# Seven block products for eight in the first matrix product of pairs of token blocks

## Chip, core and metric

One core of one Trainium2 chip. The metric is the time of the whole kernel on the device in microseconds, the median of three runs. TensorE (PE in the profile; PEld is its weight load) multiplies, VectorE (DVE), ScalarE (ACT) and GpSimd (POOL) do the elementwise work, SyncE (SP) issues the DMAs in order.

## The reference

Block-sparse attention on 4 x 8 heads of 768 tokens with 64 dimensions, and on its output a mixture of four experts, each applied to every token:

```python
scores_all = np.concatenate([scores_l_m, scores_s], axis=-1)   # window of 16, and block maxima of k
a = np.exp(scores_all - max) / (sum + 1e-09)
x = np.matmul(a, np.concatenate([v, v_sum], axis=2))           # -> (3072, 512)
p = domain_probs / (domain_probs.sum(-1, keepdims=True) + 1e-09)
for e in range(4):
    h = np.maximum(x @ w1[e], 0.0)                             # 512 -> 1024
    out += p[:, e:e + 1] * (h @ w2[e])                         # 1024 -> 512
```

Everything is float32.

## The kernel before

Tokens are cut into eight blocks of 384 (`TB`). Attention makes x transposed, in 64 steps `n` (eight for a block: four pieces of 96 queries, two groups of heads); a step is `load_piece`, `stage_a`, two `scores`, `probs`, `transposed` (a transposing DMA), `values` and `to_x`, the last of which writes x of its columns.

Matrix operands are split in two parts of type fp32r, a rounded high part and the remainder (xh and xl, wh and wl, hh and hl), and a product is three matmuls: high by high, high by low, low by high. ScalarE makes the high part, GpSimd or VectorE the low one (`split_weights`).

A pass of one expert over one or two blocks is `moe_units` (L620). Its first product, `mm1`, takes for each of 8 columns blocks `fc` of w1 (128 wide) and each token block 4 chunks of the depth (128 each) x 3 matmuls of 128x384 into one PSUM bank `ph`, 12 in all. ScalarE then takes the positive part (hh, `AF.Relu`), VectorE the remainder (hl). The second product, `mm2`, takes per 128 tokens 8 x 3 matmuls of 128x512 into a bank `po`, which VectorE scales by the expert's weight and adds to `acc`; after the fourth expert SP stores it. The pool `ps_mm` has four PSUM banks for ph and po; scores and values have two each. w1 and w2 are loaded and split anew in every pass; four w1 columns blocks and all of w2 are kept where the next pass has the same expert.

The order: `plan` (L720) has block 0 with experts 0 and 1, block 1 with experts 1 and 0, blocks 0 and 1 with experts 2 and 3, then the pairs (2,3), (4,5), (6,7) with all four experts, twelve passes in three stages. Passes give units, and after each unit `advance` lets so many attention steps be issued that they are spread evenly over the stage. The first attention steps are written out with keys of their own (`first_tokens`). Behind these the order of instructions on each engine is worked out by the planner of the tile framework, which simulates a timeline and takes what is ready by program order; tiles of one tag share a number of slots, and what needs a slot waits for the release of an earlier tile. Nearly all instructions have the line of the helper `issue`, L73, so groups are told apart by tiles.

Of the kernel before, what the change touches and what calls it, by code (L numbers as in the profile page):

```python
# [16 lines left out]
P = 128  # L17
# [19 lines left out]
LAG = 2.52  # L37
PACE = 1.013
# [4 lines left out]
STEPS = (-1.19, -0.88, 0.85, 0.66, 1.27, 1.34, 1.82, 1.84, 3.16, 3.29, 3.37, 3.66, 3.72, 5.09, 5.84, 6.11, 6.57, 6.89)  # L43
ASC = 32768.0
# [16 lines left out]
def attn_moe(ctx: ExitStack, tc: tile.TileContext, qvL, qv0, v0L, kD, kT, vT, w1L, w2L, dpL, cst, out):  # L61
# [28 lines left out]
    ps_av = pool("ps_av", 2, space=bass.MemoryType.PSUM)  # L90

# [8 lines left out]
    dp = const.tile([P, NT, E], F32, name="dp")  # L100
    pw = const.tile([P, NT, E], F32, name="pw")

    def mixing():
        SP.dma_start(dp, dpL)
        s = const.tile([P, NT, 1], F32, name="dps")
        V.tensor_reduce(s, dp, axis=AX.X, op=ALU.add)
        V.tensor_scalar_add(s, s, EPS)
        r = const.tile([P, NT, 1], F32, name="dpr")
        V.reciprocal(r, s)
        V.tensor_tensor(pw, dp, r.broadcast_to([P, NT, E]), op=ALU.mult)  # L110
# [11 lines left out]
    xT = {}  # L122
    st = {}
# [9 lines left out]
    def chunk(name):  # L133
        return sb.tile([P, S], F32, name=name, tag="chunk", bufs=2)
# [25 lines left out]
    def stack_v(b, vsr):  # L160
        vs5 = sb.tile([P, G, 5, NB], F32, name=f"vs5_{b}", tag="chunk", bufs=2)
# [8 lines left out]
        v0 = sb.tile([NST, 512], F32, name=f"v0_{b}", tag="chunk", bufs=2)  # L170
# [3 lines left out]
    def split_v(b, v0):  # L174
        b12 = sb.tile([NST, 2, 512], BF16, name=f"b12_{b}", tag="awT", bufs=2)
# [27 lines left out]
    def stage_a(n):  # L203
# [6 lines left out]
        ks = sb.tile([P, G, 2, KA], F32R, name=f"ks{n}", tag="kl", bufs=2)  # L210
        kh, kl = ks[:, :, 0, :], ks[:, :, 1, :]
        PL.tensor_copy(kr[:, :, KW:KA], ksum[b][:, h0 : h0 + G, :])
        A.copy(kh, kr)
        PL.tensor_tensor(kl, kr, kh.bitcast(F32), op=ALU.subtract)
        qs = sb.tile([P, G, QB], F32R, name=f"qs{n}", tag="qs", bufs=2)
# [10 lines left out]
    def scores(n, half):  # L226
# [17 lines left out]
        if n < APART:  # L244

            psc = ps_sc.tile([P, 2, 256], F32, name=f"psc{n}_{half}", tag="sc")
            for j in heads:
                o = psc[:QB, j % 2, :KA]
                PE.matmul(o, qs[:, j, :], ks[:, j, 0, :], start=True, stop=False)
                PE.matmul(o, qs[:, j, :], ks[:, j, 1, :], start=False, stop=True)  # L250
            for j in heads:
                maximum(j, psc[:QB, j % 2, :KA], mask)
        else:

            for j in heads:
                bank, tag = (ps_av, "av") if j == G - 1 else (ps_sc, "sc")
                o = bank.tile([P, 512], F32, name=f"psc{n}_{j}", tag=tag)[:QB, 0 : 2 * KA]
                PE.matmul(o, qs[:, j, :], ks[:, j].rearrange("p w k -> p (w k)"), start=True, stop=True)
# [8 lines left out]
    def probs(n):  # L267
        ms, rs = st[n]["ms"], st[n]["rs"]
        aw = aw_bufs[n % 2]
# [15 lines left out]
    def transposed(n):  # L285
        awT = sb.tile([P, 3 * G, QB], F16, name=f"awT{n}", tag="awT", bufs=2)
        SP.dma_start_transpose(out=awT, in_=aw_bufs[n % 2].rearrange("p a k -> p (a k)"))
        st[n]["awT"] = awT
# [27 lines left out]

    def to_x(n):
        i, g = (n // 2) % NQ, n % 2
        tb, ib = n // per, i % (TB // QB)
        if tb not in xT:  # L320
            xT[tb] = tuple(
                sb.tile([P, KC, TB], F32R, name=f"x{w}{tb}", tag=f"x{w}", bufs=4) for w in "hl"
            )
        pxv = st.pop(n)["px"]
        xh, xl = (x[:, 2 * g : 2 * g + 2, ib * QB : (ib + 1) * QB] for x in xT[tb])
# [3 lines left out]
        A.copy(xh, xs)  # L329
        PL.tensor_tensor(xl, xs, xh.bitcast(F32), op=ALU.subtract)  # L330
# [5 lines left out]
    def first_tokens(units):  # L336
        kch = [
            sb.tile([P, 2, S], F32, name=f"k0{g}", tag=("xh", "xl")[g], bufs=4) for g in range(2)
        ]
        qvs = [  # L340
            sb.tile([P, 3, 2 * (QB + 2 * D)], F32, name=f"qv0_{c}", tag=("xh", "xl")[c % 2], bufs=4)
            for c in range(3)
        ]
        vch = sb.tile([P, 2, S], F32, name="v01", tag="xl", bufs=4)
        ksr = sb.tile([P, G, NB], F32, name="ksr0", tag="ksr")
        vsr = sb.tile([P, 2, NB], F32, name="vsr0", tag="vsr")
        v0 = sb.tile([NST, 512], F32, name="v0_0", tag="chunk", bufs=2)
# [10 lines left out]
        def load_qv(m):  # L358
            n = order[m]
            SP.dma_start(qvs[m // 3][:, m % 3, :], qv0[n // 2, n % 2])  # L360

        def load_k(hp):
            load_chunk(0, hp, kch[hp // 2][:, hp % 2, :], kT)

        def load_v(g):
            if g == 1:
                for c in range(2):
                    load_chunk(0, 2 + c, vch[:, c, :], vT)
                return
# [12 lines left out]
        def k_stats(hp):  # L382
            block_stats(kch[hp // 2][:, hp % 2, :], ksr, hp, ALU.max)

        def v_means(g, key):
# [13 lines left out]
            def sums(c):  # L399
                block_stats(vch[:, c, :], vsr, c, ALU.add)  # L400
# [42 lines left out]
        def piece(n, m, s):  # L443
# [3 lines left out]
            qv = qvs[m // 3][:, m % 3, :]  # L447
# [8 lines left out]
            def scores(half):  # L456
                t["psc", half] = ps_sc.tile([P, 2, 256], F32, name=f"psc{n}_{half}", tag="sc")
                for j in (half, half + 2):
# [3 lines left out]
                        o[:, 0:KW], qr[r, j // 2, :], kch[g][r, j // 2, w0 : w0 + KW], start=True, stop=True  # L462
# [49 lines left out]
            def divide():  # L512
# [3 lines left out]
                t["xt"] = sb.tile([QB, G, D], F32, name=f"xt{n}", tag="xt", bufs=2)  # L516
# [11 lines left out]
            def x_part(w):  # L528
                xh, xl = (x[:, 2 * g : 2 * g + 2, ib * QB : (ib + 1) * QB] for x in xT[0])
# [60 lines left out]

    def load_weights(src, e, fc, which):
# [4 lines left out]
    def split_weights(raw, e, fc, which, bufs, lo_engine):  # L596
# [205 lines left out]
```

## Time and profile before

| | us |
|---|---|
| median of 3 runs (range) | 1230.19 (1229.23 to 1230.38) |
| profiled execution, its own time | 1227.44 |
| its span, first to last instruction | 1225.7 |
| PE busy | 1202.5 (98%) |
| DVE, ACT, POOL busy | 598.8 (49%), 548.8 (45%), 583.0 (48%) |
| DMA, share of 16 engines | 39.5%, 134.02 MB on the hardware queue |
| mean granted TensorE clock | 0.993 |

Busy time of PE counts a matmul from its start to the modelled end of its pipeline: 0.34 us for one of 384 columns that follows the one before at about half of that. So the distance between starts tells the pace, and the busy share tells only that there was always one under way. "Idle before" an engine's group names what ended the idle time. The clock column is the share of 2.4 GHz that was granted.

### The profile page before, as it was taken

Reading aid. Unit: us, or ns where it says so; the run is one execution under the profiler, and the core shown is the slowest. Engines: PE = TensorE matmul, PEld = TensorE weight load, DVE = VectorE, ACT = ScalarE, POOL = GpSimd, SP = SyncE. Lnnn points to the kernel's source line nnn. Section 1 sums busy time; section 2 is a strip of 40 time slices with the busy share of each in tenths; the row PEclk is TensorE's granted clock in tenths of the full one; section 3 lists DMA queues with packets and bytes.
Section 4 is the critical chain, followed back from the end, with each engine's and each line's share of the span. In section 5 each row is a group of like instructions: output and inputs, shape, how many; then the busy total and the mean of one; then the engine's idle time right before and its main releaser. Section 6 shows DMA issues by size and latency. Waiting matters only on the chain.

```text
span 1225.7 us, 19120 instructions
## 1 busy us (share of the span) xinstructions
PE 1202.5 (98%) x6829; PEld 1069.6 (87%) x6829; DVE 598.8 (49%) x1523; ACT 548.8 (45%) x1458; POOL 583.0 (48%) x574
## 2 busy tenths in 40 slices
PE   9899899999999999999999999999999999999998
PEld 7787788888989899898888989899898989899896
DVE  6878786755666545454564635545441212212121
ACT  5777567555535455454443535444440213132220
POOL 2596668756535465565534546465520213142310
PEclk9999899999999999999999999999999999999999
DMA  6578566544645244343633334244221213131201
GB/s 238 148 207 208 161 171 174 144 114 128 155 116 143 69 136 103 94 130 83 214 84 100 95 103 123 64 136 110 70 63 36 69 37 93 35 87 52 70 1 52
DMA packets 152591, 135.24 MB, mean 110 GB/s; under 512 B 77488, under 2 KB 107184, under 8 KB 152496
## 3 DMA queue, kind: packets, MB, share of 16 engines
q1 hardware_dynamic: 152496, 134.02, 39.5%
q8 instruction: 54, 0.88, 0.3%
q14 instruction: 41, 0.34, 0.1%
HBM read 110.79 MB, written 6.29 MB: 96 GB/s over the span
## 4 chain that ended last, share of the span: by engine, by line
PE 77%; DMA 1%; POOL 1%; DVE 1%; SPq 0%; issue 0%; ACT 0%; POOLq 0%; DVEq 0%
PE po L73 37%; PE ph L73 36%; PE px L73 2%; PE psc L73 2%; DMA kch<-in_kT 1%; DMA vch<-in_vT 0%; POOL wl L73 0%; SPq L73 0%; DVE ksr L73 0%; DMA ks<-ksr 0%; DVE rs L73 0%; DVE acc L73 0%; ACT ks L73 0%; POOL ks L73 0%; POOL qs L73 0%
## 5 line engine op out<-in xcount | busy, mean ns | idle before, releaser
L73 POOL TENSOR_TENSOR wl<-wr,wh 128x512 fp32r<-128x512 f32 x216 | 282.5, 1313 | 335.2 <-ACT wh L73 334.5
L73 PE MATMUL ph<-xh,wh 128*128 128x384 f32 x1024 | 351.2, 344 | 4.1 <-DVE hl L73 2.7
L73 PE MATMUL ph<-xl,wh 128*128 128x384 f32 x1024 | 349.0, 341 | 1.2 <-POOL xl L73 1.2
L73 PE MATMUL ph<-xh,wl 128*128 128x384 f32 x1024 | 348.1, 340 | 0.0
L73 PE MATMUL po<-wh,hl 128*128 128x512 f32 x768 | 304.4, 397 | 0.0
L73 PE MATMUL po<-wh,hh 128*128 128x512 f32 x768 | 302.8, 394 | 0.0
L73 PE MATMUL po<-wl,hh 128*128 128x512 f32 x768 | 301.8, 393 | 0.0
L73 ACT CAST wh<-wr 128x512 fp32r<-128x512 f32 x240 | 147.3, 618 | 255.3 <-PE po L73 90.2
L73 DVE SCALAR_TENSOR_TENSOR hl<-ph,hh 128x384 fp32r<-128x384 f32 x256 | 140.7, 553 | 210.8 <-ACT hh L73 210.4
L73 PEld LDWEIGHTS ph<-xh,wh 128*128 128x128 f32 x1024 | 193.5, 189 | 8.4 <-DVE hl L73 4.1
L73 PEld LDWEIGHTS ph<-xl,wh 128*128 128x128 f32 x1024 | 193.8, 189 | 1.9 <-POOL xl L73 1.5
L73 PEld LDWEIGHTS ph<-xh,wl 128*128 128x128 f32 x1024 | 193.5, 189 | 0.0
L73 PEld LDWEIGHTS po<-wl,hh 128*128 128x128 f32 x768 | 144.7, 188 | 32.3
L73 PEld LDWEIGHTS po<-wh,hl 128*128 128x128 f32 x768 | 144.5, 188 | 31.4
L73 PEld LDWEIGHTS po<-wh,hh 128*128 128x128 f32 x768 | 144.7, 188 | 30.7
L73 ACT ACTIVATE hh<-ph 128x384 fp32r<-128x384 f32 x256 | 123.0, 486 | 95.0 <-PE ph L73 94.9
L73 ACT ACTIVATE ms<-ms,nb 96x152 f32<-96x152 f32 x256 | 104.8, 416 | 120.6 <-DVE nb L73 119.4
L73 POOL TENSOR_TENSOR ks<-kr,ks 128x608 fp32r<-128x608 f32 x56 | 86.3, 1541 | 138.6 <-ACT ks L73 138.4
L73 DVE SCALAR_TENSOR_TENSOR acc<-po,pw,acc 128x512 f32<-128x512 f32 x72 | 52.5, 747 | 149.6 <-PE po L73 149.6
L73 DVE TENSOR_TENSOR ms<-psc,c_sb 96x152 f32<-96x152 f32 x192 | 53.0, 305 | 113.4 <-PE psc L73 113.3
L73 DVE TENSOR_TENSOR aw<-ms,aw 96x512 f16<-96x512 f32 x112 | 77.3, 725 | 13.5 <-ACT aw L73 13.3
L73 ACT CAST aw<-ms 96x512 f16<-96x512 f32 x112 | 53.3, 523 | 63.1 <-issue 30.2
(82 smaller groups left out, 1041.7 us busy)
## 6 DMA issues: line engine op xcount, KB each, us to landing
wr<-in_w1L SPq DMA_DIRECT2D x128, 256.0 KB, 2.8
wr<-in_w2L SPq DMA_DIRECT2D x112, 256.0 KB, 2.7
qv<-in_qvL SPq DMA_DIRECT2D x56, 320.0 KB, 3.3
kr<-in_kD SPq DMA_DIRECT2D x56, 256.0 KB, 2.9
out_dram<-acc SPq DMA_DIRECT2D x24, 256.0 KB, 2.0
kch<-in_kT SPq DMA_DIRECT2D x12, 384.0 KB, 3.9
vch<-in_vT SPq DMA_DIRECT2D x12, 384.0 KB, 4.0
qv<-in_qv SPq DMA_DIRECT2D x8, 224.0 KB, 5.8
```

Source lines behind the costliest of these rows:

```text
L73: ins = getattr(self.engine, name)(*a, **kw)
```

## The change

For the pairs of blocks (2,3), (4,5) and (6,7) the first product becomes `pair_units`. The two token blocks, two halves of the depth (256 each) and two neighbouring column blocks f1, f2 of w1 make a product of 2x2 blocks, and seven products (Strassen's, in Winograd's form) stand for eight. A set of seven has 7 x 2 x 3 = 42 matmuls of 128x384 into three banks a, b, c, of which a takes two products, b three and c two, added in the bank; there are four sets in a pass. Between the products the sums p1, u2 and u4 are read out and added by ScalarE and VectorE, under a raised priority (`RUSH`).

The operands of w1 (11, s2, s1, s3, 12, s4, 22 with high and low part side by side in one 128x512 tile) are made the first time, in the stage of blocks 2 and 3, and stored in device memory; later they are loaded. 14 slots (`NW1`) hold two sets. `fetch` brings the next set, two of them beside the second product (`with_fetch`); at a change of pair, where the expert is the same, two sets are kept. Attention's `to_x` writes x of these blocks to device memory, and `x_operands` loads it, makes the seven operands and splits them, in four parts issued during the second product of the last pass ahead of the pair. 14 slots with tag x serve for these, for the first tokens and, in odd attention steps below 28, for a second buffer of ks, awT and aw; ks beyond that, qs and awT have one buffer. `ENDS` gives the attention step by which each stage ends, by estimated matmul time (`US1`, `US2`) instead of units; `stage_a` is issued 0.4 step later.

```diff
-LAG = 2.52
-PACE = 1.013
+ENDS = (17.52, 25.5, 38.0, 53.0, 68.0, 70.0)
+XFREE = 28
+NX = 14
+NW1 = 14
...
+    def spare_x(n):
+        return n % 2 == 1 and n < XFREE
...
+        tag, bufs = ("x", NX) if spare_x(n) else ("kl", 2)
+        for half in range(2):
+            k2 = sb.tile([P, 2, 2, KA], F32R, name=f"ks{n}_{half}", tag=tag, bufs=bufs)
...
-        qs = sb.tile([P, G, QB], F32R, name=f"qs{n}", tag="qs", bufs=2)
+        qs = sb.tile([P, G, QB], F32R, name=f"qs{n}", tag="qs", bufs=1)
...
+        SP.dma_start(xraw[tb // 2, ib][:, 2 * g + tb % 2], xs)
...
+    XS = ("11", "21", "22", "t1", "t2", "t3", "t4")
+    def x_operands(pr):
+        xp = {w: [x_half(f"x{v}{pr}_{w}") for v in "hl"] for w in XS}
+        def split(w, raw, c, lo):
+            hi, low = (x[:, :, c : c + QB] for x in xp[w])
+            A.copy(hi, raw)
+            lo.tensor_tensor(low, raw, hi.bitcast(F32), op=ALU.subtract)
+        def part(ib):
+            raw = sb.tile([P, 4, 2, QB], F32, name=f"xr{pr}_{ib}", tag="chunk", bufs=CHUNKS)
+            SP.dma_start(raw, xraw.pop((pr, ib)))
+            b11, b12, b21, b22 = (raw[:, k] for k in range(4))
+            c = ib * QB
+            split("11", b11, c, PL)
+            V.tensor_tensor(b11, b12, b11, op=ALU.subtract)
+            split("22", b22, c, PL)
...
+            split("t4", b21, c, V)
+        return xp, [lambda ib=ib: part(ib) for ib in range(TB // QB)]
...
+    WS = ("11", "s2", "s1", "s3", "12", "s4", "22")
+    stored = {}
+    def w1_operands(e, pr):
+        ws = {w: w1_part(f"w1{w}{e}_{pr}") for w in WS}
+        if (e, pr) in stored:
+            for w in WS:
+                SP.dma_start(ws[w].bitcast(F32), stored[e, pr][w])
+            return ws
+        r1, r2 = (load_weights(w1L, e, 2 * pr + j, "1") for j in range(2))
+        a11, a12 = r1[:, 0:256], r1[:, 256:512]
+        a21, a22 = r2[:, 0:256], r2[:, 256:512]
+        def parts(w, raw, lo):
+            hi, low = ws[w][:, 0:256], ws[w][:, 256:512]
+            A.copy(hi, raw)
+            lo.tensor_tensor(low, raw, hi.bitcast(F32), op=ALU.subtract)
+            stored[e, pr][w] = dram.tile([P, 512], F32, name=f"wd{w}{e}_{pr}")
+            SP.dma_start(stored[e, pr][w], ws[w].bitcast(F32))
+        parts("11", a11, PL)
+        parts("22", a22, V)
+        PL.tensor_tensor(a22, a21, a22, op=ALU.add)
+        PL.tensor_tensor(a21, a11, a21, op=ALU.subtract)
+        PL.tensor_tensor(a11, a22, a11, op=ALU.subtract)
+        parts("s2", a11, V)
+        parts("s1", a22, PL)
+        parts("s3", a21, V)
+        parts("12", a12, PL)
+        PL.tensor_tensor(a12, a12, a11, op=ALU.subtract)
+        parts("s4", a12, V)
+        return ws
...
+    PAIRS = ((1, (3, 2, 1, 0)), (2, (0, 1, 2, 3)), (3, (3, 2, 1, 0)))
...
+    def with_fetch(units):
+        for n, us in enumerate(units):
+            if n in (1, 8):
+                fetch()
+            yield us
...
+    SEVEN = (
+        ("a", "11", "11"), ("b", "s2", "t2"), ("c", "s1", "t1"), ("b", "s3", "t3"),
+        ("a", "12", "21"), ("c", "s4", "22"), ("b", "22", "t4"),
+    )
+    def pair_units(pr, e, last=False):
...
+            for m, (k, w, x) in enumerate(SEVEN):
+                if k not in bank:
+                    bank[k] = ps_mm.tile([P, 512], F32, name=f"ph{k}{pr}_{e}_{i}", tag="mm")[:, :TB]
+                o = bank[k]
...
+                for c in range(2):
+                    again = dict(skip_group_check=k in seen)
+                    PE.matmul(o, wh[:, c, :], xh[:, c, :], start=c == 0 and k not in seen, stop=False, **again)
+                    PE.matmul(o, wh[:, c, :], xl[:, c, :], start=False, stop=False, **again)
+                    PE.matmul(o, wl[:, c, :], xh[:, c, :], start=False, stop=c == 1, **again)
...
+                ahead_of.enter_context(tc.high_priority(offset=RUSH))
+                if m == 0:
+                    A.copy(held("p1"), o)
+                elif m == 1:
+                    V.tensor_tensor(held("u2"), o, f32["p1"], op=ALU.add)
+                elif m == 2:
+                    V.tensor_tensor(held("u4"), o, f32["p1"], op=ALU.add)
+                elif m == 3:
+                    V.tensor_tensor(f32["u4"], o, f32["u4"], op=ALU.add)
+                    to_h(hT, tbs[1], e, f2, f32["u4"])
+                elif m == 4:
+                    to_h(hT, tbs[0], e, f1, o)
+                elif m == 5:
+                    V.tensor_tensor(o, o, f32["u2"], op=ALU.add)
+                    to_h(hT, tbs[1], e, f1, o)
+                else:
+                    V.tensor_tensor(o, o, f32["p1"], op=ALU.add)
+                    to_h(hT, tbs[0], e, f2, o)
...
+        yield from with_fetch(second(tbs, e, hT, w2, last))
...
-            (k - 1.0, stage_a, n),
+            (k - 0.6, stage_a, n),
```

## Rows read from the trace of the kernel before

**Rows 1.** The page of the kernel before: busy time of each engine, its share of the span and its instructions (section 1), and TensorE's busy tenths in 40 slices (section 2).

```profile
PE 1202.5 (98%) x6829; PEld 1069.6 (87%) x6829; DVE 598.8 (49%) x1523; ACT 548.8 (45%) x1458; POOL 583.0 (48%) x574
PE   9899899999999999999999999999999999999998
```


**Rows 2.** The table by stretch, cut at the first matmuls of expert passes as the TensorE timeline has them. Two single-block stages; then of the pair stages the first two passes and the last of blocks 2 and 3, the first of blocks 4 and 5, the second and the last of blocks 6 and 7. Columns: from and to, length, busy time of PE, PEld, DVE, ACT, POOL with instruction counts, granted clock, busy share of the DMA engines, GB/s.

```profile
37.00:128.00 91.00, 83.61 (x534) 72.73 (x532) 74.00 (x171) 63.05 (x181) 66.33 (x63) 0.98 0.73 199
128.00:219.00 91.00, 83.97 (x484) 73.96 (x485) 67.32 (x167) 59.01 (x163) 69.39 (x68) 0.92 0.63 169
...
370.00:443.00 73.00, 73.00 (x420) 65.27 (x419) 36.49 (x100) 36.42 (x98) 39.24 (x39) 1.00 0.44 115
443.00:515.50 72.50, 72.50 (x417) 64.78 (x416) 35.75 (x92) 34.77 (x92) 41.36 (x40) 1.00 0.39 105
...
588.00:662.70 74.70, 73.82 (x421) 65.17 (x421) 43.66 (x109) 31.15 (x88) 30.10 (x32) 1.00 0.39 111
662.70:735.50 72.80, 72.80 (x419) 65.08 (x418) 35.87 (x99) 36.40 (x98) 39.03 (x39) 1.00 0.40 110
...
1020.00:1087.20 67.20, 67.20 (x338) 60.98 (x337) 13.31 (x23) 16.90 (x32) 20.61 (x16) 1.00 0.22 63
...
1154.40:1225.70 71.30, 67.32 (x337) 60.73 (x335) 14.34 (x24) 11.12 (x22) 7.71 (x6) 1.00 0.09 33
```


**Rows 3.** The timeline in the first expert pass of blocks 6 and 7: start, duration in us, engine, operation. The first matmul of the first product, the twelfth, the consumers of that sum, the first matmul of the second product, and the first of the next pass.

```profile
952.80 0.34 PE L73 MATMUL ph<-xh,wh 128*128 128x384 f32 x1
...
954.75 0.34 PE L73 MATMUL ph<-xh,wl 128*128 128x384 f32 x1
...
955.12 0.49 ACT L73 ACTIVATE hh<-ph 128x384 fp32r<-128x384 f32 x1 [13.62 <-PE ph L73]
...
955.65 0.56 DVE L73 SCALAR_TENSOR_TENSOR hl<-ph,hh 128x384 fp32r<-128x384 f32 x1 [1.89 <-ACT hh L73]
...
986.73 0.39 PE L73 MATMUL po<-wh,hh 128*128 128x512 f32 x1
...
1019.98 0.34 PE L73 MATMUL ph<-xh,wh 128*128 128x384 f32 x1
```


**Rows 4.** VectorE's groups of instructions by line, shapes apart, in the pass from 443 to 515.5 us (expert 2 on blocks 2 and 3): busy us, mean ns of one | idle before.

```profile
L73 DVE SCALAR_TENSOR_TENSOR hl<-ph,hh 128x384 fp32r<-128x384 f32 x16 | 8.8, 552 | 13.2 <-ACT hh L73 13.2
L73 DVE TENSOR_TENSOR ms<-ms,rs 96x608 f32<-96x608 f32 x4 | 6.2, 1542 | 0.1
L73 DVE SCALAR_TENSOR_TENSOR acc<-po,pw,acc 128x512 f32<-128x512 f32 x6 | 4.4, 748 | 9.1 <-PE po L73 9.1
...
L73 DVE TENSOR_SCALAR acc<-po,pw 128x512 f32<-128x512 f32 x2 | 1.5, 740 | 0.0
```


**Rows 5.** The view of single tiles (wr, ms, ph, qv, xs), over the whole run: duration in ns, least, median and most.

```profile
L73 ACT CAST wh<-wr x240: 601/619/625, 15.1 to 1171.4; 128x512 fp32r<-128x512 f32 x120
L73 POOL TENSOR_TENSOR wl<-wr,wh x216: 1263/1293/1837, 15.7 to 1172.1; 128x512 fp32r<-128x512 f32 x108
L73 SPq DMA_DIRECT2D wr<-in_w1L x128: 327/328/684, 8.4 to 1157.6; - x128
L73 DVE TENSOR_TENSOR wl<-wr,wh x24: 676/764/1828, 38.8 to 191.4; 128x512 fp32r<-128x512 f32 x24
...
L73 DVE TENSOR_TENSOR ms<-ms,rs x56: 783/1468/1846, 59.6 to 922.2; 96x608 f32<-96x608 f32 x56
...
L73 ACT ACTIVATE hh<-ph x256: 463/486/502, 45.6 to 1188.5; 128x384 fp32r<-128x384 f32 x128
L73 DVE SCALAR_TENSOR_TENSOR hl<-ph,hh x256: 539/557/559, 46.1 to 1189.0; 128x384 fp32r<-128x384 f32 x128
...
L73 POOL TENSOR_TENSOR qv<-qv,v x56: 666/805/1303, 52.0 to 890.0; 128x256 f32<-128x256 f32 x56
...
L73 POOL TENSOR_TENSOR xl<-xs,xh x56: 589/606/1150, 76.9 to 941.6; 128x192 fp32r<-128x192 f32 x56
```


**Rows 6.** GpSimd's costliest group in the same pass, 443 to 515.5 us.

```profile
L73 POOL TENSOR_TENSOR wl<-wr,wh 128x512 fp32r<-128x512 f32 x16 | 20.7, 1294 | 15.0 <-ACT wh L73 14.9
```


**Rows 7.** The table by stretch for the first pass of blocks 6 and 7, first and second product apart; columns as in rows 2.

```profile
952.80:986.70 33.90, 33.90 (x193) 33.89 (x192) 9.32 (x17) 11.04 (x22) 9.04 (x7) 1.00 0.24 78
986.70:1020.00 33.30, 33.30 (x147) 27.08 (x146) 4.01 (x6) 4.73 (x8) 9.04 (x7) 1.00 0.19 50
```


**Rows 8.** The waits of TensorE's matmuls over the whole run: who waited for whom, us in total, times, longest.

```profile
PE psc L73 <- DVE nb L73: 6.9, 6, 3.4
PE px L73 <- DMA awT<-aw: 4.8, 4, 1.8
PE ph L73 <- DVE hl L73: 2.7, 3, 2.1
```


**Rows 9.** The longest wait of the DMA queue's own (SP), columns as in rows 8.

```profile
SPq L73 <- POOL wl L73: 402.6, 180, 18.0
```


**Rows 10.** The page's DMA issues: KB each, median us from issue to landing.

```profile
wr<-in_w1L SPq DMA_DIRECT2D x128, 256.0 KB, 2.8
```


**Rows 11.** The table by stretch from 120 to 140 us; columns as in rows 2.

```profile
120.00:130.00 10.00, 7.42 (x45) 5.59 (x39) 5.71 (x16) 5.87 (x18) 4.30 (x8) 0.98 0.70 192
130.00:140.00 10.00, 8.52 (x50) 7.89 (x51) 6.38 (x15) 3.12 (x11) 5.04 (x7) 0.68 0.68 197
```

More of the change, by code (lines that the diff above doesn't have):

```diff
@@ L122, in attn_moe @@
     xT = {}
+    xraw = {}
     st = {}
@@ L315, in values, with x_half, x_block @@
         t["px"] = pxv
+    def x_half(name):
+        return sb.tile([P, 2, TB], F32R, name=name, tag="x", bufs=NX)
+    def x_block(tb):
+        return [[x_half(f"x{w}{tb}_{g}") for w in "hl"] for g in range(2)]
     def to_x(n):
@@ L334, in attn_moe @@
     vmean0 = []
     def first_tokens(units):
[L337 to L344, printed above, removed]
+        kch = [sb.tile([P, S], F32, name=f"k0{hp}", tag="x", bufs=NX) for hp in range(4)]
+        qvs = []
@@ new lines, in attn_moe, with fetch @@
+    PAIRS = ((1, (3, 2, 1, 0)), (2, (0, 1, 2, 3)), (3, (3, 2, 1, 0)))
+    orders, todo, ready = {}, [], {}
+    before = None
+    for pr, es in PAIRS:
+        for e in es:
+            kept_pairs = orders[before][-2:] if before and before[1] == e else []
+            orders[pr, e] = kept_pairs + [i for i in range(FC // 2) if i not in kept_pairs]
+            todo += [(pr, e, i, (*before, i) if i in kept_pairs else None) for i in orders[pr, e]]
+            before = pr, e
+    def fetch(until=None):
+        while todo and until not in ready:
+            *key, same = todo.pop(0)
+            ready[tuple(key)] = ready[same] if same else w1_operands(*key[1:])
+            if until is None and not same:
+                return
@@ L621, in moe_units, with second, plain_units @@
+    def second(tbs, e, hT, w2, last):
+        whole = tbs if last else tbs[:-1]
+        for tb in whole:
+            for t in range(TB // P):
+                yield from mm2(tb, e, [t], hT, w2)
+        for tb in tbs[len(whole) :]:
+            yield from mm2(tb, e, range(TB // P), hT, w2)
+    def with_fetch(units):
[3 more added lines that the diff above has]
+            yield us
+    def plain_units(tbs, e, early=0, last=False):
         hT = {}
@@ L680, in moe_units @@
         kept[e] = {fc: w1[fc] for fc in order[-4:]}, w2
-        whole = tbs if last else tbs[:-1]
-        for tb in whole:
-            for t in range(TB // P):
-                yield from mm2(tb, [t])
-        for tb in tbs[len(whole) :]:
-            yield from mm2(tb, range(TB // P))
+        units = second(tbs, e, hT, w2, False)
+        yield from with_fetch(units) if last else units
+    SEVEN = (
+        ("a", "11", "11"), ("b", "s2", "t2"), ("c", "s1", "t1"), ("b", "s3", "t3"),
+        ("a", "12", "21"), ("c", "s4", "22"), ("b", "22", "t4"),
+    )
@@ L714, in advance @@
             at += 1
[L717 to L721 removed]
     EARLY = 4
[L723 removed]
+    ahead = plain_units([0], 0, early=EARLY)
     first_tokens(ahead)
```

272 lines of the change are left out of this document (169 added, 103 removed).

## Prediction

> **What bounds the kernel now.** I read the page's busy shares first, then the table by stretch with its cuts at the expert boundaries, then the TensorE timeline around one boundary. TensorE is busy 98% of the span, the other engines less than half [rows 1]. In the stretches of the pair stages it is busy for 100% at granted clock 1.00, but for 0.9 us in one [rows 2]. Busy is not yet work at full pace, so the pitch counts: a first product begins at 952.80 us and the second at 986.73, and the 192 matmuls between them make 0.1767 us each; the 144 of the second product run to 1019.98, 33.25 us [rows 3]. Nothing waits inside. So from 370 us on the end is set by the number of matmuls alone; VectorE, ScalarE and GpSimd are half busy (35.75, 34.77 and 41.36 of 72.5 us) while attention runs, and less behind it [rows 2]. Ahead of 219 us it is different: TensorE idles some 7 us of each 91 and was granted 0.98 and 0.92 [rows 2].
>
> **What goes.** Per expert and pair the first product has 8 x 2 x 12 = 192 matmuls; four sets of seven products have 4 x 7 x 6 = 168. 24 fewer in each of twelve passes are 288; at 0.1767 us [rows 3] that is 50.9 us of a resource that is full. The second product and attention stay. The splits of w1 for the last two pairs go from ScalarE and GpSimd too: beside TensorE, so worth nothing by themselves.
>
> **What comes, and what hides it.** A set is 42 x 0.1767 = 7.42 us. In it VectorE gets five additions and four hl. The additions are 128x384 with PSUM in them, as hl is, so I price all nine at hl's 0.55 us [rows 4]: 5.0 of 7.42 us. ScalarE gets a copy and four hh at 0.49 = 2.4 us [rows 5]. By length both fit beside TensorE. What matters is when they end, as four PSUM banks serve three running sums: the next set's a takes the free bank, its b the bank of a, its c the bank of b. A result is readable 0.37 us after its last matmul starts (954.75 to 955.12), 0.2 us after the next one starts, and an engine follows another by 0.04 us (hh ends 955.61, hl starts 955.65) [rows 3]. From a set's start:
> - the fourth product writes the second's bank at 3.18 us. The second is readable at 2.32, its addition ends at 2.87: 0.3 us to spare.
> - the next set's third product takes b's bank at 7.42 + 2.12 = 9.54. The seventh product is readable at 7.62, added by 8.17; the sixth's hl runs to 8.73, the seventh's to 9.28: 0.26 us to spare. With the sixth's hl ahead of that addition it is 10.0, 0.45 us late.
> The order is the planner's. Whatever else VectorE or ScalarE is in the middle of comes on top.
>
> *Pair 3, no attention.* Foreign are only a set's two w2 splits, 0.62 us each on ScalarE and 1.29 on GpSimd [rows 5]. Bounds 0 and 1.29 us a set (one GpSimd split holding up VectorE); I take 0.15, near the undisturbed chain: 16 x 0.15 = 2.4 us, bounds 0 to 20.6.
>
> *Pair 2.* Attention has 35.75 [rows 2] less hl 8.8, acc 4.4 and 1.5 [rows 4] = 21.0 us of VectorE for four steps, 5.3 us a step. 15 steps on four passes, 29.7 us of 63 being first product, put 0.44 step or 2.3 us into a set: 5.0 + 2.3 nearly fills 7.42. The longest single operation is 1.54 us [rows 4]. A bank is late by what is left of the operation in progress: bounds 0 and 1.54 us a set; I take 0.5, a third of the longest. Attention ends after about three passes: 12 x 0.5 + 4 x 0.15 = 6.6 us, bounds 0 to 23.6.
>
> *Pair 1* has that and makes the w1 operands: per set on GpSimd four sums and three subtractions over 256 columns at 0.80 us (qv's median; 0.67 at best [rows 5]) = 5.6 us, two w2 splits 2.6, attention 2.3 (41.36 less 20.7 for wl [rows 6], by four steps): 10.5 against 7.42, 3.1 too much. Only two sets of a pass are made under its own first product, the other two under the second product before it, where GpSimd has room. So bounds 0 and 8 x 3.1 = 25 us; I take 4, as a set's last operands are wanted 5 us after its first. With 16 x 0.5 = 8 us as in pair 2: 12 us, bounds 0 to 49.6. VectorE's four subtractions a set, some 0.41 us each by estimate (the best 512-column wl, 0.676 [rows 5], less 256 columns at 1 ns), lie inside these bounds. The 112 stores queue on SP among the loads; they are in the SP rival.
>
> *Loads.* A stored set is 7 x 256 KB = 1.84 MB. Two of four come beside the second product; with w2 the first product sees 3.7 + 2.1 MB in 29.7 us, 195 GB/s. In pair 3 78 GB/s now take 0.24 of the DMA engines [rows 7], so full is some 325; with attention's small packets, 105 GB/s at 0.39 [rows 2], some 270. It fits: 0; its bound is the third rival.
>
> *x operands.* Four parts a pair, each seven ScalarE casts of 192 columns, seven VectorE and four GpSimd operations (xl, 0.61 us [rows 5]), under a second product of 33 us: 10 to 13 us on an engine. 0; uncovered, 13 us ahead of each pair, 39 in all.
>
> *Front.* More attention comes early (8 steps for 7.1 in the second stage, 12.5 for 10 in the third), qs and awT have one buffer. TensorE's waits for attention are small in the whole run (psc for VectorE 6.9 us, px for the transposing DMA 4.8 [rows 8]) and its matmuls the same. 0, bounds -7 and +7 us, what it idles in one such stage. The end is the same last po, acc and store.
>
> **A rule weighed.** VectorE operations with both inputs in SBUF vary: ms from ms and rs takes 783, 1468, 1846 ns (least, median, most), wl on VectorE 676 to 1828, while hl, with one input in PSUM, stays within 539 to 559 [rows 5]. The Trainium skill, "SBUF — State Buffer", section "SBUF: two separate sides", has the rule: such an operation and a GpSimd operation that reads SBUF exclude each other for a whole instruction. The trace agrees: GpSimd's wl, too, goes from 1263 to 1837 [rows 5]. It speaks against this change, as the fourth product's hl now reads u4 and hh, both in SBUF. What the rows' spread would make of it is the first rival.
>
> **Sum.** 2.4 + 6.6 + 12 = 21 us given back of 50.9, 29.9 gained. From the profiled execution's 1227.44 us that is 1197.5; the median of the runs shown, 1230.19, lies 2.75 us above it, so 1200 as it will be measured.
>
> **Rivals.**
> - *Slower: VectorE held by GpSimd inside the sets.* Each two-SBUF operation adds its median excess, 1468 - 783 = 0.69 us [rows 5], to the chain of banks: five a set in pair 1 (the fourth product's hl, four w1 subtractions), one in pairs 2 and 3: 16 x 3.45 + 32 x 0.69 = 77 us, and 6 us of attention: 1230.2 - 50.9 + 83 = 1262 us. It decides from 50.9 / 48 = 1.06 us a set. For it: the spread, and how full VectorE is. Against: GpSimd is busy only 18 to 21 us of 67 in pair 3 [rows 2], and w1 is made a set ahead.
> - *All hidden.* The planner keeps the chains whole and attention drifts into the second products, where VectorE is busy 4 of 33 us without it [rows 7]: up to 5 us lost, 1179 to 1185. For it: TensorE's ph waited for hl 2.7 us in the whole run [rows 8]. Against: margins of 0.3 us.
> - *Nothing gained: the SP queue.* SP issues in order and waited 402.6 us for wl, up to 18 at once [rows 9], for nothing as long as loads are early. Now two sets a pass are fetched inside the first product, each load behind TensorE giving up its slot. Issuing seven at 0.33 us [rows 5] and landing in 2.8 [rows 10] is 5.1 us if nothing is early, of 7.42 there are; 2 us late for each of 2 x 8 - 2 = 14 sets of pairs 2 and 3 is 28 us: 1228 us, no change within 0.2%.
>
> **How the numbers follow.** Forecast (1186 to 1218 us) 0.54; all hidden 0.22; nothing gained 0.09; slower 0.15. A measurement can tell 0.2%, 2.5 us. Of the third rival 0.03 count as faster, 0.05 as the same, 0.01 as slower: faster 0.79, same 0.05, slower 0.16. The range takes in most of the hidden case and the start of the slower one: 1181 to 1236.
>
> **What would show it.** A pass of pair 3 at 63.5 us for 67.2; of pair 2 70.5 for 72.7; of pair 1 71.5. TensorE's new waits should name VectorE (additions, hl) in pair 2, and the w1 tiles besides in pair 1. I am wrong if TensorE waits for loads, if the first 370 us move by more than 7, or if the clock falls behind 370 us: it was 0.68 from 130 to 140 us, after 10 us with TensorE busy for 7.42 [rows 11].

## The result and the profile after

The changed kernel takes 1241.44 us (median of 4 runs, 1237.98 to 1242.37) against 1230.29 (4 runs, 1229.23 to 1230.61) on the same chip: a ratio of 1.0087 with a 95% interval of 1.0066 to 1.0108, so it is slower by 0.9%. The forecast was 1200 and the range ended at 1236. The profiled execution took 1240.75 us with a span of 1238.8, against 1225.7 before.

The page after, busy time by engine and TensorE's slices; it answers to [rows 1]:

```profile
PE 1170.8 (95%) x6541; PEld 1023.4 (83%) x6541; DVE 762.0 (62%) x1911; ACT 574.3 (46%) x1626; POOL 588.9 (48%) x658
PE   9899799999989899998989989999999999999998
DVE  5876778665888958839499473654716351515151
```

The matmuls are gone: 6829 - 6541 = 288 fewer, as forecast, and TensorE is busy for 31.7 us less. But the span grew by 13.1. So what TensorE does was cut and what it waits for grew. VectorE has 163 us more work in 388 more instructions; no other engine gained more than 26. Its slices reach 8 and 9 between the 11th and the 22nd (310 to 680 us), and TensorE's line has six 8s from the 12th to the 24th, where before it had none [rows 1].

The table by stretch after, with the cuts at the first matmuls of passes as before, columns as in [rows 2]: the third stage in two passes (experts 2 and 3 on blocks 0 and 1), then four passes each of the three pairs.

```profile
224.70:301.90 77.20, 75.85 (x461) 67.13 (x460) 48.62 (x136) 48.44 (x143) 52.20 (x57) 1.00 0.53 137
301.90:392.06 90.16, 79.65 (x461) 68.82 (x460) 73.11 (x185) 50.14 (x160) 58.38 (x72) 0.96 0.71 205
392.06:469.40 77.34, 73.47 (x430) 63.60 (x429) 59.15 (x164) 47.80 (x148) 58.58 (x67) 0.98 0.73 217
469.40:544.40 75.00, 72.32 (x392) 61.39 (x391) 51.40 (x132) 40.76 (x120) 55.59 (x61) 0.98 0.70 209
544.40:621.50 77.10, 71.56 (x381) 61.40 (x380) 56.19 (x133) 38.98 (x112) 48.41 (x55) 0.98 0.74 238
621.50:700.30 78.80, 72.47 (x395) 63.56 (x394) 63.76 (x164) 43.70 (x138) 50.92 (x61) 0.96 0.54 160
700.30:776.80 76.50, 71.63 (x394) 61.89 (x393) 40.94 (x115) 32.72 (x91) 28.03 (x31) 0.98 0.62 179
776.80:849.80 73.00, 69.90 (x392) 60.21 (x391) 37.77 (x107) 31.08 (x86) 27.12 (x30) 1.00 0.63 181
849.80:922.40 72.60, 70.04 (x407) 60.79 (x406) 37.90 (x107) 29.10 (x79) 21.44 (x22) 1.00 0.60 168
922.40:985.30 62.90, 62.67 (x314) 56.13 (x313) 33.04 (x71) 18.46 (x49) 11.59 (x18) 1.00 0.29 93
985.30:1047.70 62.40, 62.40 (x314) 56.18 (x313) 23.31 (x43) 13.71 (x27) 8.89 (x7) 1.00 0.49 156
```

The passes of the pair of blocks 6 and 7 take 62.4 us for 67.2, and nothing in them waits: VectorE is busy 23.3 of 62.4. The four passes of the first pair take 77.3, 75.0, 77.1 and 78.8 for the 72.7 to 74.6 that they took before, though each has 24 matmuls fewer; VectorE is busy 51 to 64 us there, where it was at 36 [rows 2], and the clock shows 0.96 to 0.98 where it was 1.00. The second pair stands between. The last pass ahead of the pairs takes 90.2 us. Cut at the stages, between the two kernels' first matmuls:

| | before | after | difference | forecast |
|---|---|---|---|---|
| to the first pair | 369.9 | 392.1 | +22.2 | 0 |
| blocks 2, 3 | 292.8 | 308.2 | +15.4 | -5.0 |
| blocks 4, 5 | 290.1 | 285.0 | -5.1 | -10.4 |
| blocks 6, 7, with the end | 272.9 | 253.5 | -19.4 | -14.6 |
| span | 1225.7 | 1238.8 | +13.1 | -29.9 |

(The forecast of a pair is its term given back less a third of 50.9.) 22 of the 43 us between forecast and result arose ahead of the pairs, 20 in the first pair, 5 in the second; the third gave 5 back.

TensorE's waits after over the whole run, columns as in [rows 8]:

```profile
PE px L76 <- DMA awT<-aw: 18.6, 16, 3.4
PE phc L76 <- DVE hl L76: 8.2, 7, 2.7
...
PE phb L76 <- DVE u L76: 4.5, 3, 1.9
```

The same in the passes of blocks 2 and 3 alone, 392.06 to 700.3 us:

```profile
PE phc L76 <- DVE hl L76: 5.2, 3, 2.7
PE phb L76 <- DVE u L76: 4.5, 3, 1.9
PE phb L76 <- DVE hl L76: 2.8, 5, 0.9
PE pha L76 <- DVE hl L76: 2.2, 1, 2.2
```

In the first pair the four longest name VectorE and the banks a, b, c; the kernel before has 0.9 us of waits in its passes of these blocks. None names a w1 tile. Over the whole run the longest sum is attention's transposing DMA, 18.6 us for 4.8 before [rows 8]; 9.8 of it lie ahead of the pairs, 2.0 in the first pair and 6.8 in the second, where it is more than the 3.9 us of waits for hl. The timeline around one wait of 2.7 us shows what such a line is made of (start, duration, engine, operation; in brackets the idle time before):

```profile
656.03 0.49 ACT L76 ACTIVATE hh<-phc 128x384 fp32r<-128x384 f32 x1
...
656.22 0.55 DVE L76 TENSOR_TENSOR phb<-phb,p 128x384 f32<-128x384 f32 x1
...
656.69 0.36 DVE L76 TENSOR_TENSOR xr<-xr 128x192 f32<-128x192 f32 x1
...
656.79 1.38 POOL L76 TENSOR_TENSOR wl<-wr,wh 128x512 fp32r<-128x512 f32 x1
656.97 1.42 DVE L76 TENSOR_TENSOR aw<-ms,aw 96x192 f16<-96x192 f32 x1
...
658.31 0.30 DVE L76 CUSTOM_DVE_ANT_0 ms<-psc,ms 96x152 f32<-96x152 f32 x1
...
658.55 0.30 DVE L76 TENSOR_TENSOR ms<-psc,c_sb 96x152 f32<-96x152 f32 x1
...
658.78 0.51 DVE L76 TENSOR_TENSOR xr<-xr 128x192 f32<-128x192 f32 x1
...
659.21 0.55 DVE L76 SCALAR_TENSOR_TENSOR hl<-phc,hh 128x384 fp32r<-128x384 f32 x1
...
659.81 0.59 PE L76 MATMUL phc<-xh_t,w1s 128*128 128x384 f32 x1 [2.68 <-DVE hl L76]
```

hh of bank c is there at 656.52 us. Its hl could run then, but on VectorE stand ahead of it, in this order, a sum of the set (already under way), an x operand for the next pair, attention's aw, two of its ms and a second x operand; hl starts at 659.21, and TensorE gets the bank at 659.81. None of them is long but aw, which took 1.42 us while GpSimd's wl was under way. One of the same size took 0.53 us at 559.87, and there too GpSimd had an operation under way, by the trace until 560.17:

```profile
558.90 1.27 POOL L76 TENSOR_TENSOR ks<-kr,ks 128x304 fp32r<-128x304 f32 x1
...
559.87 0.53 DVE L76 TENSOR_TENSOR aw<-ms,aw 96x192 f16<-96x192 f32 x1
```

The prediction priced "what is left of the operation in progress"; here it was a queue of six operations.

How full VectorE was shows when a pass is cut at the last matmul of its first product. The lines are the second pass of the first pair, first and second product, and the first product of the second pass of the second pair, columns as in [rows 2]:

```profile
469.42:513.86 44.44, 41.76 (x251) 37.16 (x249) 39.80 (x111) 32.77 (x100) 39.90 (x46) 0.96 0.79 221
513.86:544.42 30.56, 30.56 (x143) 24.23 (x143) 11.59 (x22) 7.97 (x20) 15.69 (x17) 1.00 0.57 191
...
776.78:820.31 43.53, 40.43 (x264) 36.20 (x263) 31.96 (x91) 24.48 (x71) 17.37 (x22) 1.00 0.89 256
```

In the four first products of the first pair VectorE is busy for 39.0 to 46.7 of 44.1 to 48.5 us, 9.8 to 11.7 us a set, and in the second products for 11.6 to 20.1 of 29.6 to 33.3. In the first three first products of the second pair it is busy for 30.5 to 32.4 of 42.6 to 44.4 us, 7.6 to 8.1 a set.

### The profile page after: what moved, and what is told of

It reads as the page before. It is cut to its first block, busy times and chain, and to the rows that moved or that the text cites. A ratio compares the mean times of both kernels' runs of the same rounds, so it can differ in the third digit from the quotient of the medians.

```text
span 1238.8 us, 20130 instructions
## 1 busy us (share of the span) xinstructions
PE 1170.8 (95%) x6541; PEld 1023.4 (83%) x6541; DVE 762.0 (62%) x1911; ACT 574.3 (46%) x1626; POOL 588.9 (48%) x658
## 4 chain that ended last, share of the span: by engine, by line
PE 68%; DVE 11%; DMA 9%; POOL 5%; issue 3%; ACT 3%; SPq 1%; POOLq 0%; ACTq 0%; DVEq 0%
PE po L76 36%; PE phb L76 9%; PE phc L76 6%; PE pha L76 6%; PE ph L76 4%; DMA awT<-aw 3%; DMA wr<-in_w1L 2%; PE psc L76 2%; DVE ms L76 2%; POOL wl L76 2%; PE px L76 2%; DVE hl L76 2%; DVE aw L76 2%; PE pav L76 1%; DVE w1s L76 1%
## 5 line engine op out<-in xcount | busy, mean ns | idle before, releaser
L76 POOL TENSOR_TENSOR wl<-wr,wh 128x512 fp32r<-128x512 f32 x132 | 178.4, 1356 | 320.9 <-ACT wh L76 313.3
L76 ACT CAST wh<-wr 128x512 fp32r<-128x512 f32 x156 | 95.4, 618 | 198.2 <-PE po L76 152.9
L76 POOL TENSOR_TENSOR ks<-kr,ks 128x304 fp32r<-128x304 f32 x112 | 105.3, 946 | 66.4 <-ACT ks L76 65.2
L76 PE MATMUL phb<-xh_t,w1s 128*128 128x384 f32 x384 | 118.8, 350 | 8.3 <-DVE u L76 4.5
L76 PE MATMUL pha<-xh,w 128*128 128x384 f32 x384 | 114.3, 342 | 2.6 <-DVE hl L76 2.2
L76 PE MATMUL ph<-xh,wh 128*128 128x384 f32 x256 | 88.3, 352 | 6.9 <-ACT xh L76 3.5
L76 PE MATMUL ph<-xh,wl 128*128 128x384 f32 x256 | 88.4, 345 | 4.8 <-POOL wl L76 4.8
L76 DVE TENSOR_TENSOR aw<-ms,aw 96x512 f16<-96x512 f32 x112 | 84.9, 785 | 11.6 <-ACT aw L76 10.8
L76 PE MATMUL ph<-xl,wh 128*128 128x384 f32 x256 | 88.3, 345 | 0.0
L76 PEld LDWEIGHTS phb<-xh_t,w1s 128*128 128x128 f32 x384 | 72.8, 193 | 13.5 <-DVE hl L76 6.2
L76 PEld LDWEIGHTS pha<-xh,w 128*128 128x128 f32 x384 | 71.9, 191 | 4.4 <-DVE hl L76 2.5
```

Of the source, the lines that this page charges most:

```text
L76: ins = getattr(self.engine, name)(*a, **kw)
```

## The experiments

All runs but one (the seven products in the last pair only) were executed once. Executions of one kernel differ by some us (four of the changed kernel lie between 1237.98 and 1242.37, eight of the kernel before on one chip between 1226.01 and 1231.19), so a difference of 2 or 3 us between single runs shows nothing. The pair stages are compared by the span less the start of the first pair: 855.8 us before, 846.7 after.

**Making the w1 operands, attention, and both.** In two runs all sets after the first are loaded:

```diff
-        if (e, pr) in stored:
+        if stored:
             for w in WS:
-                SP.dma_start(ws[w].bitcast(F32), stored[e, pr][w])
+                SP.dma_start(ws[w].bitcast(F32), stored[3, 0][w])
```

and in two the attention steps of blocks 4 to 7 are left out:

```diff
...
-    for n in range(per, NTB * per):
+    for n in range(per, 4 * per):
...
```

> The changed kernel, but only the first set of w1 operands is made and stored; every other set, of the pair of blocks 2 and 3 too, is loaded from that one stored set (15 of 16 makings left out, so the products are not the reference's). Theory M (the making of w1 operands is what the passes of blocks 2 and 3 lose by): these passes fall from 75 to 79 us to 71 to 73 us, as those of blocks 4 and 5, and the whole run from 1241 to about 1220 us. Theory A (attention and the seven products share VectorE and the in-order queues, the making matters little): the passes stay at 74 us or more, the run at 1230 to 1238 us.

> The changed kernel without the 32 attention steps of blocks 4 to 7; x of these blocks is taken from blocks 2 and 3 (left out: half of attention). Theory A: every pass of the pairs takes 62.4 us as those of blocks 6 and 7 do now, 749 us for twelve, and the run about 1140 us. Theory M: passes of blocks 2 and 3 keep most of their excess, 68 us or more, those of blocks 4 and 5 are at 62.4, the run at 1160 us or more.

> Both left out, the makings of e1 and the attention of e2. Both theories: all passes 62.4 us, the run about 1135 to 1140 us. If passes stay longer, it is the loads of operands or the x operands that hold TensorE, which neither theory has.

Spans: 1221.1 us with w1 loaded, 1135.4 without the later attention, 1126.4 with neither. The pair stages alone: 836.2, 761.2 and 753.9. Passes of the first pair in the second run and in the third, columns as in [rows 2]:

```profile
374.20:437.80 63.60, 63.17 (x314) 56.07 (x313) 30.14 (x59) 20.88 (x52) 26.68 (x32) 1.00 0.53 178
437.80:502.00 64.20, 63.62 (x314) 55.89 (x313) 31.70 (x59) 23.29 (x56) 32.20 (x36) 1.00 0.54 180
```

```profile
372.50:434.90 62.40, 62.40 (x313) 56.18 (x312) 23.19 (x43) 13.68 (x27) 8.91 (x7) 1.00 0.51 156
```

Twelve passes of 62.4 and 4 us of end are 752.8: without attention and without making, the seven products run at TensorE's pace in all three pairs, loads included. Making alone adds 761.2 - 753.9 = 7.3 us in the pairs; beside attention 846.7 - 836.2 = 10.5. With w1 loaded the whole run came near what theory M gave, but 7.2 of its 17.7 us were gained ahead of the pairs, and the passes of the first pair did not: 74.7, 72.5, 73.8 and 80.2 us, 301.3 in all for 308.2. So making is not most of what that pair lost. The first product of its second pass:

```profile
459.66:503.06 43.40, 40.84 (x268) 36.90 (x267) 36.60 (x105) 27.24 (x84) 21.14 (x25) 1.00 0.98 261
```

VectorE is busy 36.6 us there, 9.2 a set, with no w1 operand to make.

Attention adds 761.2 to 846.7, 85.5 us (82.3 where w1 is loaded); in the kernel before it adds only 855.8 - (12 x 67.2 + 4.1) = 45.3. That difference, some 40 us, lies between attention and the seven products themselves, and is the larger part of what went wrong in the pairs. It is rather more than 40, as the changed kernel has moved some attention steps ahead of the pairs.

**The buffers and the pace alone.** The kernel before with the changed kernel's attention buffers (one qs and awT, ks in halves) and its `ENDS`:

```diff
...
-        qs = sb.tile([P, G, QB], F32R, name=f"qs{n}", tag="qs", bufs=2)
...
+        qs = sb.tile([P, G, QB], F32R, name=f"qs{n}", tag="qs", bufs=1)
...
-    for tbs, experts, goal in plan:
+    ENDS = (17.52, 25.5, 38.0, 53.0, 68.0, 70.0)
+    for (tbs, experts, goal), end in zip(plan, ENDS):
...
-        end = goal - 1 + LAG
...
```

> The kernel before, eight products, with the attention buffers of the changed one (one qs, one awT and one aw for steps from 28 on and for even steps, ks in halves, second buffers for odd steps below 28) and its attention pace (17.52, 25.5, 38, 53, 68). Theory B (the buffers and the pulled-ahead attention alone cost what is lost up to 392 us and part of the pairs): 1245 to 1255 us, the third stage 10 us or more longer than 151, TensorE waiting for awT and for psc banks in the pairs. Theory A: 1228 to 1236 us, no new waits behind 370 us.

1235.77 us beside 1230.63 for the kernel before on that chip: 5 us. Pairs begin at 376.3 for 369.9, and the pair stages take 857.7 for 855.8. So this is a small part, nearly all of it ahead of the pairs; TensorE's wait for awT is 5.9 us in the whole run, near the 4.8 of [rows 8], so beside eight products the single buffers don't make the 18.6.

**VectorE's additions, or the SP queue.** Two runs set the sums (theory V) against the transposes behind the loads on SP (theory S); a third gives GpSimd attention's larger low part from step 38 on. The edits:

```diff
-                if m == 0:
-                    A.copy(held("p1"), o)
-                elif m == 1:
-                    V.tensor_tensor(held("u2"), o, f32["p1"], op=ALU.add)
...
+                if m == 3:
+                    to_h(hT, tbs[1], e, f2, o)
...
```

```diff
-        SP.dma_start_transpose(out=awT, ...
+        A.dma_start_transpose(out=awT, ...
```

```diff
-        V.tensor_tensor(aw[:, G : 2 * G, :], ms[:, :, 0:KW], aw[:, 0:G, :], op=ALU.subtract)
+        (PL if n >= 38 else V).tensor_tensor(aw[:, G : 2 * G, :], ...
```

> The changed kernel with its 42 matmuls a set and its attention, but without the five additions and the copy p1 between the products (left out: the sums, so h is not the reference's); four hh and four hl remain, from the banks. Theory V (VectorE's additions, between which attention's operations come to stand, are what TensorE waits for in the pairs): excess in the passes with attention falls by more than half, passes of blocks 2 and 3 to 70 to 73 us, of 4 and 5 to 68 to 71, the run to 1205 to 1215 us. Theory S (SP: the transposing DMAs of attention queue behind loads and stores of operands that wait for slots): the waits of px for awT stay, and the run stays above 1225 us.

> The changed kernel with the transposing DMA of awT issued by ScalarE's queue instead of SP's; nothing is left out. Theory S: the waits of px for awT (18.6 us in the run) all but go, the run is 10 to 20 us faster than 1241 us. Theory V: those waits go or not, VectorE stays the one waited for, the run is within 6 us of 1241.

> The changed kernel with the larger of the two subtractions that make the low part of aw (0.9 us on VectorE) done by GpSimd for steps from 38 on; nothing is left out. Theory V: VectorE has 0.9 us less in each of 26 steps, and TensorE waits 5 to 12 us less in the pairs: 1229 to 1236 us. Theory S or the length of attention's chain: no change or slower, since GpSimd takes longer for it.

Without the sums 1199.1 us. Its table by stretch for the first pair, and all of TensorE's waits there:

```profile
387.40:459.40 72.00, 71.44 (x431) 62.30 (x430) 52.90 (x144) 45.37 (x144) 55.54 (x67) 1.00 0.77 235
459.40:528.50 69.10, 68.25 (x378) 59.90 (x377) 39.54 (x102) 35.76 (x106) 47.56 (x56) 1.00 0.74 218
528.50:599.10 70.60, 70.60 (x397) 60.47 (x396) 47.97 (x118) 40.05 (x117) 52.02 (x60) 1.00 0.83 263
```

```profile
PE pha L76 <- DVE hl L76: 1.4, 1, 1.4
PE po L76 <- DVE hl L76: 0.8, 1, 0.8
PE px L76 <- DMA awT<-aw: 0.6, 1, 0.6
PE phb L76 <- DVE hl L76: 0.3, 1, 0.3
```

The pair stages fall from 846.7 to 809.9 us, by 36.8: nearly the 40 of the first group. The clock is 1.00 in all three lines, and in the second pair no wait is left at all. With the sums the waits for awT in the pairs go too, from 8.8 to 0.6 us, though SP has the same loads; ahead of the pairs, where there are no sums, 8.0 of 9.8 stay. ScalarE lost its 48 copies of p1 as well, and a bank of a set is no longer read out between two of its products; this run doesn't tell these from VectorE's work. The waits named VectorE. With the transposes on ScalarE's queue the time is 1266.9 us, 25 worse and outside what either theory gave, and TensorE waits longer for awT:

```profile
PE px L76 <- DMA awT<-aw: 45.2, 25, 5.1
```

That alone doesn't clear SP, as in this run the transposes stand among ScalarE's own work. The run without sums speaks against SP: it has the same loads there. That the input of the transposes is late, behind the sums, fits it. But with w1 loaded, where VectorE has less to do, these waits are 14.1 us in the pairs for 8.8, so the loads may have a share that no run takes apart. GpSimd in VectorE's place gave 1244.93 us, no gain, where theory V had 1229 to 1236:

```profile
463.70:547.40 83.70, 73.87 (x383) 62.26 (x383) 55.82 (x130) 40.69 (x120) 57.92 (x66) 0.96 0.64 193
```

Where w1 is made the passes got longer, this one most (83.7 us for 75.0; the pair 320.3 for 308.2); the pair behind it took 282.3 us for 285.0. In the first product of the pass shown GpSimd had been busy 39.9 of 44.4 us already, so it has little room to give there.

**Seven products in the last pair only.** What the first group left standing is the stage without attention. The kernel before keeps its buffers and its way through blocks 2 to 5; blocks 6 and 7 get the seven products, the w1 operands made there once and not stored, in slots that w1 and attention leave free, and attention ends earlier, at step 69:

```diff
+    LATE = 6
...
+    EARLIER = 69.0
...
+        if tbs[0] == LATE - 2:
+            end = EARLIER
...
+            if tbs[0] == LATE:
+                units = pair_units(e, last=e == experts[-1])
+            else:
+                units, ahead = ahead or moe_units(tbs, e), None
```

> The kernel before, with the seven products in the stage of blocks 6 and 7 alone, where no attention is left. Its w1 operands are made there once and not stored; the attention of blocks 6 and 7 ends some 2 steps earlier in the stage of blocks 4 and 5, and their x operands are made under its last second product; attention's buffers are those of the kernel before. Nothing is left out. If it is the overlap of attention and seven products that costs: passes of blocks 6 and 7 take 62.4 to 64 us instead of 67.2, the stages ahead are within 4 us of those before, and the run takes 1211 to 1220 us. If making w1 operands (2 us a pass in e2) or x operands cost more where they stand now, 1220 to 1230 us.

1220.14 us (median of 5 runs, 1219.69 to 1224.35) against 1228.76 (8 runs): a ratio of 0.9943, 0.9919 to 0.9966. It is faster than both kernels, and lies at the border between the two outcomes expected of it. Its table by stretch for the last pass of blocks 4 and 5 and the first two of 6 and 7:

```profile
884.50:953.90 69.40, 69.40 (x372) 62.18 (x372) 31.19 (x69) 25.35 (x69) 25.50 (x31) 1.00 0.22 69
953.90:1017.50 63.60, 63.10 (x313) 56.59 (x312) 29.33 (x59) 22.03 (x52) 26.68 (x32) 1.00 0.19 63
1017.50:1083.70 66.20, 64.07 (x313) 56.26 (x312) 30.30 (x59) 23.72 (x56) 31.23 (x36) 1.00 0.22 64
```

The pair takes 264.5 us (953.9 to the end of the span, 1218.4) for the 272.9 before: 8 of the 19 us that the changed kernel saves there. The rest, 1.2 to 3.8 us a pass in these two, goes with making the operands there (VectorE 29 to 30 us for 23, GpSimd 27 to 31 for 9); in the changed kernel they come loaded.

**Ahead of the pairs.** The last pass there, 90.2 us for 74.3, had the x operands of the first pair, two sets of w1 and more attention. The x operands of that pair are loaded instead of made; in a second run w1 besides:

```diff
+            if pr == 1:
+                src = xraw.pop((pr, ib)).rearrange("p k g s -> p (k g s)")
+                tiles = [x for w in XS for x in xp[w]]
+                for x in tiles[ib::4]:
+                    SP.dma_start(x.rearrange("p c s -> p (c s)").bitcast(F32), src)
+                return
```

> The changed kernel, except that the x operands of the first pair (blocks 2 and 3) are not made: their 14 tiles are loaded with attention's raw x of these blocks, so the sums and splits of x_operands are left out there (the output is not x's). The other pairs make theirs. Theory X (the x operands, issued on VectorE beside attention in the last pass ahead of the pair, cost most of what that pass grew, from 74 to 90 us): that pass falls to 75 to 79 us, the first pair begins at 377 to 381 us and the span falls by 10 to 15 us. Rival (buffers, pace and the two sets of w1 operands cost it): the pass stays above 85 us and the pair begins after 387 us; the span falls by less than 5 us.

> The kernel with w1 operands loaded (one set made, all others loaded from it) and, in addition, the x operands of the first pair loaded raw as in the run before: w1 sums and splits and the first pair's x sums and splits are left out. What is left in the stages ahead of the pairs is the changed buffers, the pace and the additional attention steps. If the parts add up, the pair begins at 370 to 375 us, within 6 us of the kernel before's 369.9, and the span is 10 to 15 us below that of the run with w1 loaded alone (1221). If the parts do not add (one cover hides the other), the pair begins at 380 us or later.

```profile
301.40:381.10 79.70, 76.28 (x458) 66.41 (x457) 56.23 (x153) 42.03 (x131) 45.95 (x57) 1.00 0.91 258
```

The pass falls from 90.2 to 79.7 us, VectorE in it from 73.1 to 56.2, the clock rises from 0.96 to 1.00, and the first pair begins at 381.1. By that theory X holds, nearly. But the span falls by 5.4 us only, to 1233.4, where 10 to 15 were expected: about half of the 11 us is spent again in the pairs, which took 852.3 us; why, one run doesn't tell. With w1 loaded as well the first pair begins at 378.7, between the two limits that I had set, and the span is 1216.8, 4.3 us below that of w1 alone, again less than the 10 to 15 expected. So of the 22.2 us ahead of the pairs 8.8 remain (6.4 of them the buffers and the pace of the fourth run), and x and w1 hold 13.4 together: 11.0 and 7.2 if taken away singly, less than their sum, which fits each giving room to the other.

## Why the prediction was wrong

- **What bounds, and what goes: right.** 288 matmuls went, and where nothing else is added they are worth even more than 0.1767 us each (67.2 - 62.4 = 4.8 us for 24). Where TensorE is full, the number of matmuls does set the time.
- **Pair 3, 2.4 us given back: right in kind.** 63.5 us a pass were forecast, 62.4 measured. The chains of banks with margins of 0.3 us hold when only they are on VectorE: the sums took 0.558 us each as priced.
- **Pair 1, "I take 4" for making and "16 x 0.5 = 8 us as in pair 2": the step that failed.** 12 us were to be given back, 8 of them waits behind one operation in progress; 32.4 were (15.4 lost besides the 17.0 of the matmuls). The runs show 36.8 us for the sums in all pairs; with the sums gone the pass is 69 to 72 us. The step took the queue ahead of an hl to be one operation long, bounds 0 and 1.54 us. By the prediction's own numbers VectorE had 5.0 of 7.42 us a set in sums and hl, 2.3 in attention and 4 x 0.41 = 1.6 in w1 subtractions, named last and put "inside these bounds": 8.9 of 7.42 us. The trace shows 9.8 to 11.7 us a set, part of it let in by the longer product itself. So the queue grows through a first product and empties in the second, while the chains of banks end inside each set. I had summed VectorE for pair 2, "nearly fills", and GpSimd for pair 1, but not VectorE for pair 1. The w1 subtractions are the smaller part: with w1 loaded the same sum is 7.3 us, but 9.2 a set were measured, as the work beside sums and hl, attention's above all, was some 4 us a set and not 2.3; and the pair still took 301.3 us for 292.8 before. What a filled VectorE does and what the longer chain of banks does by itself was not taken apart; alone, in pair 3, the chain costs nothing.
- **What is late next: not followed.** VectorE makes attention's weights too. When they are late, awT is, and TensorE, in order, waits at attention's matmuls: 8.8 us in the pairs, 0.6 without the sums; that the loads have no share in it is not shown. The granted clock in the first pair was 0.96 to 0.98 where it had been 1.00, in passes where TensorE idled; it was named as a sign of being wrong, without a price. By the table's clocks and lengths (0.02, 0.02, 0.02 and 0.04 of the four passes) an estimate is some 8 us of TensorE's time in that pair, beside 14.7 us in the four longest waits.
- **Pair 2, 6.6 us: too small.** Its bound was 23.6. Its four passes are 76.5, 73.0, 72.6 and 62.9 for 70.5 forecast; the last is shorter because attention has ended. 5 of the 10 us expected of it are missing. More in truth: by the count of xs on VectorE 26 of attention's steps lie ahead of the pairs, 17 in the first and 13 in the second, where it was 24, 16 and 16. At 45.3 us for the 32 steps in the pairs before, an estimate of 1.4 us a step, some 4 of the 5 us that this pair saved are steps done earlier, and some 3 of the 22.2 us ahead of the pairs.
- **x operands 0, front 0 within 7: the second step that failed.** "10 to 13 us on an engine under a second product of 33 us" left out that attention was in the same pass and engine, with more steps than before: VectorE was busy 41.1 of the 47.4 us from 344.7 on, where the parts are issued, and of the 10.3 us that TensorE's matmuls wait in that pass 8.4 name VectorE's part of attention:

```profile
344.70:392.06 47.36, 40.77 (x209) 32.18 (x206) 41.09 (x104) 27.07 (x90) 31.36 (x39) 0.93 0.60 172
```

  The bound of 13 us ahead of a pair holds for the first: 11.0 were found. For pairs 2 and 3 it was not measured alone; the pass ahead of pair 2 takes 78.8 us, 1.5 to 3.8 more than the three before it, the one ahead of pair 3, where attention has ended, 62.9.
- **Loads 0: right.** DMA engines are busy for 0.73 in the first pair and TensorE has no wait for a w1 tile; all loads and no attention is 62.4 us a pass. The third rival (SP) falls with it: its 28 us of late w1 loads are nowhere.
- **The first rival, slower by VectorE and GpSimd excluding each other: the right side, by another mechanism.** 1262 was 20 too much. The rule of the Trainium skill ("SBUF — State Buffer", "SBUF: two separate sides"), that such a VectorE operation and a GpSimd operation that reads SBUF block each other, finds single rows for it, as the aw of 1.42 us above, and one that doesn't fit it, the aw of 0.53 beside ks. In the sum it is small: the operation that I priced it by, ms from ms and rs, has a median of 959 ns after for 1468 before, and hl from u, with both inputs in SBUF, one of 550, against 544 with one input in PSUM; a few long ones bring its 48 to 29.6 us in all, against 26.1 for the 48 from bank c:

```profile
L76 DVE TENSOR_TENSOR ms<-ms,rs x56: 771/959/1873, 61.0 to 885.8; 96x608 f32<-96x608 f32 x56
L76 DVE SCALAR_TENSOR_TENSOR hl<-u,hh x48: 541/550/1068, 401.8 to 1200.9; 128x384 fp32r<-128x384 f32 x48
L76 DVE SCALAR_TENSOR_TENSOR hl<-phc,hh x48: 537/544/548, 403.6 to 1206.3; 128x384 fp32r<-128x384 f32 x48
```

  What the rows can't say is how much of VectorE's filling in the first pair the stretched ones make; no run here takes them out alone.

## What to carry to other kernels

Fewer matmuls are paid for by the engine that empties the banks: add up its work per set, foreign work on the same queue included, and where the sum comes near the set's time or passes it, don't count on the matmuls saved there: here it was 7.6 to 11.7 us for 7.42, and they bought little or less than nothing. A saving like this one is applied stage by stage, first where that engine is idle: in the pair without attention it gave 19 us with operands loaded and 8 with operands made, and beside attention it cost more than it saved in the first pair and saved 5 us in the second, most of them attention done earlier. Preparing operands "under" another product is free only if the engine that prepares has room in that very pass, and what one takes away there is not additive.

## What the runs showed that was not expected

First products of seven run at a smaller pitch. In the timeline of the third pair the matmuls from 985.26 us to 1012.31 are 156 of 128x384 with nothing between, 0.1734 us each against 0.1767 [rows 3]; that is 0.55 us of each pass, and why the third pair gained more than 24 x 0.1767. Nothing here tells the cause.

```profile
985.26 0.33 PE L76 MATMUL pha<-xh,w 128*128 128x384 f32 x1
985.43 0.34 PE L76 MATMUL pha<-xl,w 128*128 128x384 f32 x1
```

A transposing DMA occupies the queue that issues it for longer than I had in mind: 1.30 us by median on SP, and 1.31 on ScalarE in the run that moved it there, against 0.33 for a plain load [rows 5].

```profile
L76 SPq DMA_TRANSPOSE awT<-aw x56: 1251/1304/3006, 67.9 to 888.2; - x56
```
